# Decayed attention and a gated FFN on one core: a build-time list scheduler, q, k and x turned by DMA, paired heads, and a first batch in two parts

## The chip, the cores and the metric

The kernel runs on one core of one Trainium2 chip. Its time is the device time of one execution in microseconds (us). Every run below was timed together with runs of the kernel before on the same chip. "Span" is the length of the one execution that was profiled; it is some 2 us shorter than its time.

The names in the profile: PE is the matrix engine (TensorE) and PEld its weight loads, DVE is VectorE, ACT is ScalarE, POOL is GpSimd, SP is SyncE. "SPq" in a line of the profile stands for SP's queue, on which DMAs are issued.

## The reference, cut to what matters

```python
# q, k, v: [8 batches, 8 heads, 576 tokens, 64]; f: [8, 8, 576]
scores = scale * q @ k.T
decay  = cum[:, :, :, None] - cum[:, :, None, :]      # cum = cumsum(log f)
attn   = softmax(where(causal, -1e9, scores + decay))
x      = (attn @ v).transpose(0, 2, 1, 3).reshape(4608, 512)
xn     = x / sqrt(mean(x * x) + 1e-6) * rms_g
out    = (silu(xn @ w_gate) * (xn @ w_val)) @ w_out    # 512 -> 1536 -> 512
```

Attention of one batch must be done before the FFN can work on its 576 tokens. The FFN has groups of 512 tokens, so a batch's rows feed two groups.

## The kernel before

q and k arrive as [tokens, heads x 64] and have to be turned (transposed), so that the 64 features of a head lie on the partitions. PE does it, 128x128 at a time, and DVE copies the result out of PSUM. x is turned in the same way after the norm. Scores are made head by head, one 512-column bank at a time.

```python
def transposes(b, p):
    for src, store, nm in ((qb[b % 2], QT, "QT"), (kb[b % 2], KT, "KT")):
        tp = ps_tr.tile([128, NB * 128], BF16, name="tr")
        for j in range(NB):
            nc.tensor.transpose(tp[:, j * 128:(j + 1) * 128], src[:, j, p * 128:(p + 1) * 128], ident)
        t = store[b, p] = qkt.tile([128, NB * 128], BF16, name=f"{nm}{p}")
        nc.vector.tensor_copy(t, tp)

def scores(b, p, bank):
    for par in range(2):                       # the two heads of pair p
        # ... (cut)
        rows = slice(par * 64, par * 64 + 64)
        sc = ps_sc.tile([128, 512], F32, name="sc")
        for kj, q0, n, c in BANKS[bank]:
            nc.tensor.matmul(sc[:, c:c + n], lhsT=KT[b, p][rows, kj * 128:(kj + 1) * 128],
                             rhs=QT[b, p][rows, q0:q0 + n], start=True, stop=True)
        t = PT[b, h]
        nc.scalar.activation(t[:, bank * 512:(bank + 1) * 512], sc, ACT.Exp, scale=scale)
        # ... causal masks on POOL (cut)

def norm(b):
    # ... squares of the 5 row blocks on ACT, rs = (mean + eps) ** -0.5 on POOL (cut)
    for j in range(NB):
        nc.vector.tensor_scalar_mul(xn[:, j, :], x[:, j, :], rs[:, j:j + 1])
```

The order of the work is that of the program. All of batch 0's attention comes first. After it the attention pieces of batches 1 to 7 are spread between the FFN pieces by an estimate of their cost:

```python
for _, work in attention(0):
    work()
# ... stream = attention pieces of batches 1 to 7 with a cost each (cut)
for work in ffn:
    n += 1
    want = lead + total_a * n / (slots + LEAD)
    while i < len(stream) and done_a < want:
        done_a += stream[i][0]
        stream[i][1]()
        i += 1
    work[1]()
```

The softmax here doesn't subtract the row's maximum and nothing guards it: scores larger than these inputs give would overflow.

## Time and profile before

The time was 487.32 us (median of 3 runs, 486.21 to 487.49), and the profiled span 484.0 us. First four lines of the page of the kernel before: the engines' busy time, and then one digit for each of 40 equal slices of the span (12.1 us each). A digit is the busy share in tenths; in the PEclk line it is the granted clock of PE in tenths of full speed.

```profile
PE 423.9 (88%) x3317; PEld 207.6 (43%) x3317; DVE 260.3 (54%) x534; ACT 222.1 (46%) x436; POOL 187.7 (39%) x335
...
PE   0491707999999999999999999999999999999996
...
PEclk9999999999999999999999999999999999999999
DMA  9999991594190419041903290010001000201102
```

After the seventh slice PE is busy without a break. In the first six it is mostly idle, while the DMA engines are full. The view by stretches gives the same in numbers. Its columns are the stretch, its length, the busy time (and count) of PE, PEld, DVE, ACT and POOL, the granted clock, the DMA engines' mean load, and GB/s.

```profile
0.00:74.00 74.00, 28.48 (x239) 15.88 (x239) 17.75 (x49) 21.26 (x40) 57.63 (x95) 1.00 1.48 177
100.00:436.00 336.00, 327.60 (x2663) 160.06 (x2662) 209.16 (x426) 174.76 (x350) 119.37 (x221) 1.00 0.37 52
```

From 100 to 436 us PE is busy 327.6 of 336 us (97.5%): it is the bound there, and only less PE work can shorten it. In the first 74 us PE works 28.5 us. Its timeline shows how the head ends, and what attention costs PE later. A line has the start, the length, engine, line, operation, tiles, shapes and count, and in brackets the idle time before it with what ended it.

```profile
59.40 0.93 PE L231 MATMUL po<-Vs_104,PT 128*128 128x65 bf16 x14 [0.90 <-DVE x L235]
...
72.66 0.29 PE L258 MATMUL tr<-ident,xn 128*128 128x128 bf16 x1 [10.45 <-DVE xn L252]
...
75.89 0.58 PE L296 MATMUL ff<-xT,wg 128*128 128x512 bf16 x1 [0.58 <-DVE xT L265]
...
230.37 0.58 PE L202 MATMUL sc<-QT_2664,KT_2672 64*128 64x512 bf16 x2
...
235.50 0.59 PE L231 MATMUL po<-Vs_104,PT 128*128 128x65 bf16 x14
...
236.05 0.39 PE L202 MATMUL sc<-QT_2695,KT_2703 64*128 64x512 bf16 x2
```

The first FFN matmul is at 75.89 us, after PE waited 10.45 us for the normed rows of batch 0. Deep in the run two score banks of one pair (one 512-column matmul for each head) take 0.58 us at 230.37 us, where they run one after the other, and 0.39 us at 236.05 us, where they overlap.

**How PE time is split in this document.** I count the work of PE as each matmul's columns divided by 2.4, plus 2.5, in ns, and score matmuls of two paired heads as half, because they can run side by side. (Five small float32 matmuls at the start are counted four times, 0.4 us in all.) This is an estimate. The Trainium skill (TensorE: Matmul & The Clock Gate, Back-to-back issue gap) has this formula for isolated matmuls, and the trace of before agrees: 28 matmuls of 512 columns in a row took 6.04 us, 0.2157 us each. (For a stream of matmuls the same section gives about 131 ns at 512 columns; the trace doesn't show that.) Elapsed time less this work is called *loss*. For the kernel before, work is 279.7 (FFN) + 77.8 (attention) = 357.5 us, and the loss is 484.0 - 357.5 = 126.5 us: 82.8 before 140 us, 25.8 from 140 to 320 us, and 17.9 after that.

### The profile page before, as it was taken

The numbers are of one execution on the slowest core, as the hardware profiler recorded it, in microseconds if no ns is written. First come the engines' busy times: TensorE is split into PE (matmuls) and PEld (weight loads), VectorE is DVE, ScalarE is ACT, GpSimd is POOL, SyncE is SP. The second block draws the span as 40 slices with busy tenths as digits, with TensorE's granted clock in tenths as the row PEclk, the third lists the DMA queues.
The fourth block names the chain that finished last, engine by engine and source line by source line (L and its number), as shares of the span: only waits on it lengthen the run. The fifth ranks groups of instructions, "written<-read, shape, count | busy, mean of one in ns | idle before, by whom it ended". The sixth has DMA issues, their size and how long they took to land.

```text
span 484.0 us, 8505 instructions
## 1 busy us (share of the span) xinstructions
PE 423.9 (88%) x3317; PEld 207.6 (43%) x3317; DVE 260.3 (54%) x534; ACT 222.1 (46%) x436; POOL 187.7 (39%) x335
## 2 busy tenths in 40 slices
PE   0491707999999999999999999999999999999996
PEld 0231403454544454445444544454444544444442
DVE  3210326478447844784478457745774577373670
ACT  3060321664465437544754474447444744232321
POOL 8539990665182518252825282513111211000000
PEclk9999999999999999999999999999999999999999
DMA  9999991594190419041903290010001000201102
GB/s 151 175 195 178 191 187 33 36 65 99 65 120 3 100 66 119 3 100 67 120 1 77 70 118 0 1 66 23 3 0 66 23 1 0 88 1 45 43 1 87
DMA packets 123080, 33.73 MB, mean 70 GB/s; under 512 B 113760, under 2 KB 118368, under 8 KB 123040
## 3 DMA queue, kind: packets, MB, share of 16 engines
q0 software_dynamic: 79744, 14.16, 36.6%
q1 hardware_dynamic: 43296, 19.03, 14.9%
q8 instruction: 26, 0.43, 0.4%
q14 instruction: 14, 0.11, 0.1%
HBM read 37.90 MB, written 9.44 MB: 98 GB/s over the span
## 4 chain that ended last, share of the span: by engine, by line
PE 67%; POOL 13%; issue 6%; DMA 6%; ACT 5%; DVE 2%; POOLq 0%; ACTq 0%
PE ff L311 20%; PE ff L296 14%; PE ff L304 13%; PE sc L202 7%; PE po L231 5%; PE tr L167 4%; DMA wv<-in_moe_w_val_dram 3%; PE tr L258 3%; POOL Vs_104 L160 2%; DMA qb_100<-in_q_dram 2%; ACT junk L245 2%; POOL Vs_105 L160 2%; POOL rs L249 2%; ACT PT L205 2%; POOL qb_100 L77 2%
## 5 line engine op out<-in xcount | busy, mean ns | idle before, releaser
L205 ACT ACTIVATE PT<-sc 128x512 bf16<-128x512 f32 x192 | 105.1, 599 | 87.6 <-PE sc L202 73.8
L296 PE MATMUL ff<-xT,wg 128*128 128x512 bf16 x432 | 114.7, 382 | 0.7 <-DVE xT L265 0.6
L304 PE MATMUL ff<-xT,wv 128*128 128x512 bf16 x432 | 114.0, 380 | 0.0
L311 PE MATMUL ff<-wo,hT 128*128 128x512 bf16 x432 | 112.5, 380 | 0.0
L301 DVE SCALAR_TENSOR_TENSOR ga<-th,ff 128x512 f32<-128x512 f32 x108 | 74.2, 687 | 66.9 <-ACT th L299 66.3
L299 ACT ACTIVATE th<-ff 128x512 f32<-128x512 f32 x108 | 64.5, 598 | 82.6 <-PE ff L296 80.9
L306 DVE SCALAR_TENSOR_TENSOR hT<-ga,ff 128x512 bf16<-128x512 f32 x108 | 74.2, 687 | 9.0 <-PE ff L304 0.3
L304 PEld LDWEIGHTS <-wv 128*128 128x128 bf16 x432 | 42.2, 98 | 50.2 <-issue 2.5
L208 POOL TENSOR_SCALAR_AFFINE_SELECT PT<-PT 128x128 bf16<-128x128 bf16 x64 | 19.1, 299 | 97.8 <-ACT PT L205 97.6
L296 PEld LDWEIGHTS <-wg 128*128 128x128 bf16 x432 | 38.6, 98 | 42.0 <-issue 5.6
L314 ACT COPY ores<-ff 128x512 f32<-128x512 f32 x36 | 21.1, 586 | 75.2 <-PE ff L311 74.4
L213 POOL TENSOR_SCALAR_AFFINE_SELECT PT<-PT 128x384 bf16<-128x384 bf16 x64 | 33.0, 528 | 53.2 <-ACT PT L205 53.1
L311 PEld LDWEIGHTS <-hT 128*128 128x128 bf16 x432 | 36.5, 98 | 36.4 <-issue 9.5
L231 PEld LDWEIGHTS <-PT 128*128 128x128 bf16 x896 | 35.7, 102 | 31.2 <-POOL PT L208 9.7
L234 DVE RECIPROCAL rden<-po 128x5 f32<-128x5 f32 x64 | 12.2, 191 | 55.3 <-PE po L231 55.3
L258 PE MATMUL tr<-ident,xn 128*128 128x128 bf16 x160 | 20.6, 229 | 18.3 <-DVE xn L252 18.0
L231 PE MATMUL po<-Vs_104,PT 128*128 128x65 bf16 x448 | 22.7, 206 | 13.6 <-POOL PT L208 9.2
L235 DVE TENSOR_TENSOR x<-po,rden 128x320 f32<-128x320 f32 x64 | 31.4, 490 | 1.7
L245 ACT ACTIVATE junk<-x 128x512 bf16<-128x512 f32 x40 | 25.0, 624 | 9.0 <-DVE x L235 8.4
L258 PEld LDWEIGHTS <-xn 128*128 128x128 bf16 x160 | 12.4, 100 | 37.0 <-DVE xn L252 29.1
L265 DVE TENSOR_SCALAR xT<-tr,rg 128x512 bf16<-128x512 bf16 (+7 forms) x64 | 20.5, 362 | 12.3 <-PE tr L258 12.1
L252 DVE TENSOR_SCALAR xn<-x,rs 128x512 bf16<-128x512 f32 x40 | 18.1, 520 | 13.2 <-POOL rs L249 13.2
(300 smaller groups left out, 387.8 us busy)
## 6 DMA issues: line engine op xcount, KB each, us to landing
out_dram<-ores SPq DMA_DIRECT2D x36, 256.0 KB, 2.0
qb_100<-in_q_dram POOLq DMA_DIRECT2D x16, 128.0 KB, 5.3
kb_102<-in_k_dram POOLq DMA_DIRECT2D x16, 128.0 KB, 5.4
qb_101<-in_q_dram POOLq DMA_DIRECT2D x16, 128.0 KB, 4.4
kb_103<-in_k_dram POOLq DMA_DIRECT2D x16, 128.0 KB, 4.5
wg<-in_moe_w_gate_dram POOLq DMA_DIRECT2D x3, 512.0 KB, 12.7
wv<-in_moe_w_val_dram POOLq DMA_DIRECT2D x3, 512.0 KB, 14.0
wo<-in_moe_w_out_dram POOLq DMA_DIRECT2D x2, 768.0 KB, 12.3
```

Of the source, the lines that this page charges most:

```text
L202: nc.tensor.matmul(sc[:, c:c + n], lhsT=KT[b, p][rows, kj * 128:(kj + 1) * 128], rhs=QT[b, p][rows, q0:q0 + n], start=True, stop=True)
L205: nc.scalar.activation(t[:, bank * 512:(bank + 1) * 512], sc, ACT.Exp, scale=scale)
L213: nc.gpsimd.affine_select(out=d, in_=d, pattern=[[0, 3], [1, 128]], compare_op=ALU.is_ge, fill=0.0, base=0, channel_multiplier=-1)
L231: nc.tensor.matmul(po[:, qi, :], lhsT=weights_of(b, h, qi, kj), rhs=Vs[b % 2][:, kj, h, :], start=(kj == 0), stop=(kj == qi))
L245: nc.scalar.activation(junk, x[:, j, :], ACT.Square, accum_out=sq[:, j:j + 1])
L258: nc.tensor.transpose(tp[:, j * 128:(j + 1) * 128], xn[:, j, dc * 128:(dc + 1) * 128], ident)
L296: nc.tensor.matmul(pg, lhsT=wg[:, dc, fc * 128:(fc + 1) * 128], rhs=xT[:, dc, :], start=(dc == 0), stop=(dc == NDC - 1))
L299: nc.scalar.activation(t, pg, ACT.Tanh, scale=0.5)
L301: nc.vector.scalar_tensor_tensor(a, in0=t, scalar=1.0, in1=pg, op0=ALU.add, op1=ALU.mult)
L304: nc.tensor.matmul(pv, lhsT=wv[:, dc, fc * 128:(fc + 1) * 128], rhs=xT[:, dc, :], start=(dc == 0), stop=(dc == NDC - 1))
L306: nc.vector.scalar_tensor_tensor(hTs[g][:, fc, :], in0=a, scalar=0.5, in1=pv, op0=ALU.mult, op1=ALU.mult)
L311: nc.tensor.matmul(po, lhsT=hTs[g][:, fc, j * 128:(j + 1) * 128], rhs=wo[:, fc, :], start=(fc == 0), stop=(fc == NFC - 1))
```

## The change

The intent: give PE less to do in the middle, and start the FFN sooner. The diff rewrites the kernel; these are its main parts.

1. All work is cut into pieces, each with an engine, a duration, dependencies and buffers. A list scheduler simulates the run at build time, and the program is written in the simulated order.
2. q and k (batches 1 to 7) and x are turned by DMAs that transpose, issued on SP's queue. Only batch 0 is still turned by PE (`PE_TURN`).
3. Two heads are made in one visit, with their matmuls alternating, and one exponential covers both (1024 columns).
4. The first batch is split in two parts, and the first two groups have 256 tokens, so that the FFN can begin on its first 256.

```diff
-LEAD = 6
+LEAD, UNTIL = 34.0, 0.85
+SPLIT, PE_TURN = (0,), (0,)
+GROUPS = ((0, 256), (256, 512)) + tuple((a, a + 512) for a in range(512, B * S, 512))
+LOAD_AHEAD, LOAD_LATE, SV_PRIO = -1.6, 0.3, -0.7
 ... (cut)
+class Plan:
+    def run(self):                     # a simulation in time; pieces go out in order of p.start
 ... (cut)
+        if e == "PE":
+            behind = a_done < self.lead + (a_total - self.lead) * min(1.0, f_done / (f_total * self.until))
+            first = "A" if behind else "F"                  # attention or FFN first
+            p = min(c, key=lambda p: (p.kind != first, p.prio))
 ... (cut)
+        dma_free = max(dma_free, p.start + 0.4 * p.dur) + p.xfer
+        p.done = max(dma_free, p.end) + 1.7
 ... (cut)
-            nc.tensor.transpose(tp[:, j * 128:(j + 1) * 128], src[:, j, p * 128:(p + 1) * 128], ident)
-        nc.vector.tensor_copy(t, tp)
+        def turn_dma(nm, j):
+            nc.sync.dma_start_transpose(out=QK[i][:, :, "qk".index(nm), j * 128:j * 128 + n],
+                                        in_=T[nm, b, j][0:n, :])
+        c = plan.add(key, "SP", 1.25 if j < 4 else 0.7, ..., xfer=0.8 if j < 4 else 0.4, ...)
 ... (cut)
+        for p, (c0, blocks, _) in visit:                    # two banks a visit
+            sc = ps_sc.tile([128, 2, 512], F32, name="sc", tag="sc")
+            for kj, q0, n, c in blocks:
+                for par in range(2):
+                    nc.tensor.matmul(sc[:, par, c:c + n], lhsT=QK[i][r, p, 1, ...], rhs=QK[i][r, p, 0, ...])
+        nc.scalar.activation(T["pt", b, p][:, :, c0:c0 + n], sc[:, :, 0:n], ACT.Exp, scale=scale)
 ... (cut)
+            nc.vector.scalar_tensor_tensor(xn, in0=x[:, j, :], scalar=rs[:, j:j + 1], in1=rgb, ...)
 ... (cut)
+with tc.manual_schedule():
+    for p in plan.run():
+        p.fn()
```

`UNTIL` is the share of the FFN over which attention is spread: at 0.85, the last attention piece is due when 85% of the FFN is done.

## The prediction

> **What bounds it now.** The span is 484.0 us (timed 487.3). By stretches: from 0 to 74 us PE is busy 28.5 us only and no FFN matmul runs (the timeline has the first at 75.9 us); DMA is saturated (share 1.48), POOL busy 57.6 us with load issues (0.88 us each), V scaling and masks; the waits show PE and ACT waiting for POOL masks (9.2 and 12.6 us) and PE for the first xn (11.3 us). From 100 to 436 us PE is busy 97.5% at full clock: it is the bound. There one batch takes 48.0 us (195 to 243), of which FFN is 144 matmuls of 512 columns at 0.2157 us (28 in a row: 6.04 us) = 31.1 us, so attention costs PE 16.9 us.
>
> **What the change does to PE.**
> - Turning q, k, x by DMA takes 60 PE transposes a batch away: groups of five cost 0.28 to 0.38 us in the timeline, so 4 to 4.5 us, plus about 1 us of waits for xn.
> - Paired heads: where both heads are adjacent now, two banks take 0.32 us; apart, each takes 0.32. The Trainium skill (TensorEngine Tiling, Overview) says that 64-row contractions can run as two independent tiles; the trace agrees where they meet. Two paired banks a visit: 2 x 0.213 + 0.1 = 0.53 us, six visits: 3.2 us a batch against about 6.
> - Values stay: 0.46 us a head, 3.7 us. The last corner: 0.25 us.
> So attention is about 7.2 us a batch for 1 to 7, saving 9.7 x 7 = 68 us on the critical engine. PE's sum: 280 (FFN) + 8 x 7.2 + about 5 (batch 0's transposes and split) = 343 us.
>
> **Head.** 256-token groups and the split batch let FFN begin about 25 us; weights (landing by about 35 us now) pace group 0. Groups 0 and 1 are 31 us of PE. Group 2 needs batch 1: loads land about 55 us, its 12 exponentials of about 1.04 us (two 0.6 us ones joined) bound that stretch, with some of batch 2's, so group 2 begins about 80 us. PE idle up to there: 26 to 32 us (45 now).
>
> **Costs added.** About 16 DMA transposes a batch on SP's queue (HWDGE only, by the skill's DMA: Bandwidth & Descriptors, DMA Transpose; no trace shows one yet). I take 1 to 1.5 us each: 16 to 24 us of SP in a 39 us batch. Loads now take a DMA share of 0.56 of 48 us = 27 us, so the queues are near full; SP in order may hold back v loads and stores. ACT (26 us), DVE (25) and POOL (22) fit in 39 us.
>
> **Sum.** By 82 us PE has done about 54 of 343 us; 289 remain, plus 3% of stalls (9) and 4 us of last copy and store: span 384, timed 388 us. Range 368 to 422. Faster by over 2%: 0.95; within 2%: 0.02; slower: 0.03.
>
> **Right or wrong in the profile.** PE instructions fall from 3317 to about 3030; no PE transposes after 60 us; over 95% busy PE in slices from 85 us on; two-bank score visits about 0.53 us; first FFN matmul at 22 to 32 us; idle PE between groups 1 and 2, released by ACT exponentials or DMA transposes; DMA transposes landing in 2 to 4 us.
>
> **What would make it wrong.** DMA transposes of 3 us or more each on SP, which would make the queue the bound (130 x 3 = 390 us); PE waiting on DMA or POOL in mid-span because the build-time order misses the real durations; score pairs not overlapping (plus 20 us); a starved start (FFN after 40 us).

## The result, and the profile after

| | kernel before | kernel after |
|---|---|---|
| time, median (5 runs) | 487.14 us (486.21 to 487.49) | 444.67 us (442.0 to 445.16) |
| span of the profiled run | 484.0 us | 440.3 us |
| PE work, as estimated above | 357.5 us | 334.1 us |
| loss up to 140 us / 140 to 320 us / 320 us to the end | 82.8 / 25.8 / 17.9 us | 74.4 / 9.3 / 22.6 us |

The ratio is 0.9129, with a 95% interval of 0.9102 to 0.9155. Ratios and intervals in this document are from the fast runs of the same rounds; they are not quite the ratio of the medians. The change saves 42.5 us; the prediction was 388 us, with 422 us as the upper end. Of the 43.7 us of span, 23.4 us is less PE work and 20.3 us is less loss. The work is mostly the transposes that PE no longer does (e5 below, which gives them back to PE, has 21.2 us more). What pairing brings is part of the loss, since the estimate counts score matmuls as half in both kernels.

The same four lines of the page of the kernel after (a slice is 11.0 us here), and one line from its list of DMA issues (tiles, queue, operation, count, median us from issue to landing):

```profile
PE 372.5 (85%) x3033; PEld 195.8 (44%) x3033; DVE 236.0 (54%) x446; ACT 213.3 (48%) x351; POOL 191.3 (43%) x283
...
PE   0468829974589999998999999999999952999996
...
PEclk9999968995589999999999999999999985899999
DMA  9999999999999999999990621100220112101002
...
QK<-ld SPq DMA_TRANSPOSE x70, 4.4
```

PE begins sooner, but falls back twice in the head, in the sixth slice and from the ninth to the eleventh, and there is a new hole near the end (the 5 and the 2). The DMA engines are full for 21 slices, up to 231 us, where before they were full for six and then in bursts. The 70 DMA transposes of q and k are new, and land 4.4 us after their issue in the median of the whole run. The view by stretches of the kernel after:

```profile
0.00:127.00 127.00, 80.13 (x892) 53.94 (x893) 55.76 (x140) 60.65 (x99) 97.44 (x150) 0.87 1.64 158
127.00:340.00 213.00, 209.39 (x1692) 103.43 (x1689) 137.44 (x239) 121.45 (x200) 90.36 (x130) 1.00 0.81 105
340.00:380.00 40.00, 26.56 (x198) 13.10 (x197) 13.27 (x26) 13.95 (x24) 3.54 (x4) 0.79 0.18 42
```

The middle is 98% busy, as hoped. PE's timeline of the kernel after, head, middle and tail:

```profile
37.05 1.04 PE L670 MATMUL ff<-xT,wg 128*128 128x256 bf16 x4
...
63.56 1.27 PE L577 MATMUL ff<-ident,xn 128*128 128x128 bf16 x8 [5.84 <-DVE xn L552]
...
81.57 0.61 PE L495 MATMUL sc<-QK 64*128 64x128 bf16 x8
...
119.29 0.93 PE L524 MATMUL po<-Vs,PT 128*128 128x65 bf16 x14 [3.08 <-DVE x L533]
...
127.08 1.03 PE L670 MATMUL ff<-xT,wg 128*128 128x512 bf16 x4
...
252.10 0.61 PE L495 MATMUL sc<-QK 64*128 64x128 bf16 x8
252.64 1.04 PE L670 MATMUL ff<-xT,wv 128*128 128x512 bf16 x4
...
371.68 1.87 PE L670 MATMUL ff<-xT,wg 128*128 128x512 bf16 x4 [9.29 <-issue]
```

The FFN begins at 37.05 us instead of 75.89. Batch 1's first scores are at 81.57 us, and group 2, the first that needs batch 1 (the first gate matmul of 512 columns), begins at 127.08 us. Up to there PE has done 53.8 us of work and lost 73.3 us, to waits as the 3.08 us before 119.29 and to slow matmuls as those of that line (14 value matmuls in 0.93 us). In the middle, a visit of two paired banks takes from 252.10 to 252.64 us, so 0.54 us up to the next matmul. At the end PE waits 9.29 us before 371.68 us and then runs four gate matmuls in 1.87 us instead of 1.04: at half clock.

What held batch 1? SP's queue in the timeline of the kernel after (a run of issues is one line; its second number is the time from the first one's start to the last one's end):

```profile
42.41 3.70 SPq L440 DMA_TRANSPOSE QK<-ld  x2
...
49.58 16.00 SPq L440 DMA_TRANSPOSE QK<-ld  x5
...
66.29 9.57 SPq L440 DMA_TRANSPOSE QK<-ld  x4
...
116.55 7.84 SPq L571 DMA_TRANSPOSE xT<-xn  x6
```

Batch 1's ten q and k loads are issued on POOL from 25.6 to 49.1 us, and land 10.8 to 16.9 us later. The transposes that follow them then take 16.00 us for five and 9.57 us for four on SP, and land 7.3 to 14.2 us after their issue in this stretch (median 9.4). That is why the first scores are at 81.57 us: the last block that they need lands at 78.6 us. From 40 to 180 us SP's queue has few gaps: DMA issues fill 34.8 of 40, 46.5 of 50 and 46.4 of 50 us (40 to 80, 80 to 130 and 130 to 180 us). Batch 1's attention ends at 105.4 us (its last product on DVE), and DVE starts on its first normed rows at 111.90 us. The six transposes of its x come on SP only at 116.55 us, behind nine of batch 3's q and k, and take 7.84 us; the four that group 2 needs have landed by 126.3 us, and then it begins.

The clock matters too. The Trainium skill (TensorE: Matmul & The Clock Gate, Part 1) says that the granted clock falls to half after an idle window of about 3.4 us and comes back after a busy one. The clock record of the kernel after agrees on the length of the window: it has three stretches at 0.50, from 59.1, 100.0 and 359.5 us, of 10.2, 23.9 and 17.1 us, which are 3, 7 and 5 times 3.41 us, and in them matmuls take about twice as long. It differs on "idle": the second and the third began before PE's long waits. In the 3.41 us ahead of each PE had been busy 42% and 47% of the time, with no gap longer than 1 us:

```profile
96.63:100.04 3.41, 1.45 (x32) 1.01 (x32) 0.69 (x2) 3.32 (x4) 2.77 (x4) 1.00 1.73 191
356.04:359.45 3.41, 1.59 (x40) 1.22 (x39) 1.37 (x4) 2.01 (x3) 1.51 (x2) 1.00 0.00 0
```

So short gaps close together were enough here to lose the clock. By the estimate above the three stretches cost 11.9 us in all. Before 38.6 us the trace holds no clock event, and the views show 1.00; but there matmuls are as slow as at half clock (four gate matmuls of 256 columns at 37.05 us take 1.04 us, and 0.60 us at 79.95 us), which costs some 6.6 us more by the same estimate. It is not all a cost of the change: the kernel before ran its head at half clock as well (0.93 us against 0.59 us for 14 value matmuls, shown above), some 10.8 us up to its first clock event at 79.4 us.

### The profile page after: what moved, and what is told of

The parts are those of the page before. It is cut to its first block, busy times and chain, and to the rows that moved or that the text cites. A ratio compares the mean times of both kernels' runs of the same rounds, so it can differ in the third digit from the quotient of the medians.

```text
span 440.3 us, 7998 instructions
## 1 busy us (share of the span) xinstructions
PE 372.5 (85%) x3033; PEld 195.8 (44%) x3033; DVE 236.0 (54%) x446; ACT 213.3 (48%) x351; POOL 191.3 (43%) x283
## 3 DMA queue, kind: packets, MB, share of 16 engines
q1 hardware_dynamic: 94912, 31.69, 42.0%
## 4 chain that ended last, share of the span: by engine, by line
PE 63%; DVE 9%; DMA 9%; POOL 7%; issue 6%; ACT 3%; SPq 2%; POOLq 0%; DVEq 0%; ACTq 0%
PE ff L670 33%; PE ff L691 20%; PE po L524 6%; PE sc L495 3%; DVE xn L552 3%; DMA ld<-in_q_dram 3%; DMA v<-in_v_dram 3%; DVE x L533 2%; DVE ga L679 2%; POOL Vs L367 2%; DMA ld<-in_k_dram 2%; DVE hT L685 2%; SPq L440 1%; DMA out_dram<-ores 1%; POOL ld L349 1%
## 5 line engine op out<-in xcount | busy, mean ns | idle before, releaser
L670 PE MATMUL ff<-xT,wg 128*128 128x512 bf16 (+1 forms) x480 | 116.0, 365 | 9.9 <-issue 9.3
L670 PE MATMUL ff<-xT,wv 128*128 128x512 bf16 (+1 forms) x480 | 115.1, 363 | 2.8 <-DVE ga L679 2.6
L675 ACT ACTIVATE th<-ff 128x512 f32<-128x512 f32 (+1 forms) x120 | 66.4, 554 | 96.0 <-PE ff L670 93.3
L503 ACT ACTIVATE PT<-sc 128x1024 bf16<-128x1024 f32 (+2 forms) x100 | 94.6, 989 | 36.0 <-PE sc L495 35.2
L679 DVE SCALAR_TENSOR_TENSOR ga<-th,ff 128x512 f32<-128x512 f32 (+1 forms) x120 | 75.8, 631 | 61.1 <-ACT th L675 60.6
L511 POOL TENSOR_SCALAR_AFFINE_SELECT PT<-PT 128x1024 bf16<-128x1024 bf16 (+1 forms) x44 | 37.8, 872 | 120.3 <-ACT PT L503 119.7
L685 DVE SCALAR_TENSOR_TENSOR hT<-ga,ff 128x512 bf16<-128x512 f32 (+1 forms) x120 | 76.1, 634 | 18.7 <-PE ff L670 6.8
L524 PE MATMUL po<-Vs,PT 128*128 128x65 bf16 x896 | 43.2, 202 | 17.5 <-DVE x L533 16.3
L552 DVE SCALAR_TENSOR_TENSOR xn<-x,rs,rgb 128x512 bf16<-128x512 f32 x40 | 35.4, 928 | 31.4 <-POOL rs L548 31.4
L495 PE MATMUL sc<-QK 64*128 64x64 bf16 (+3 forms) x584 | 35.9, 257 | 10.7 <-ACT PT L503 7.1
L349 POOL DMA_DIRECT2D ld<-in_k_dram x40 | 34.8, 870 | 6.9 <-DMA QK<-ld 5.2
## 6 DMA issues: line engine op xcount, KB each, us to landing
wo<-in_moe_w_out_dram POOLq DMA_DIRECT2D x2, 768.0 KB, 18.1
```

What stands on the lines that cost most here:

```text
L349: nc.gpsimd.dma_start(out=t[0:block(j), :].rearrange("p (h d) -> p h d", d=D), in_=src[b, :, j * 128:j * 128 + block(j), :].rearrange("h p ...
L495: nc.tensor.matmul(sc[:, par, c:c + n], lhsT=QK[i][r, p, 1, kj * 128:(kj + 1) * 128], rhs=QK[i][r, p, 0, q0:q0 + n], start=True, stop=True)
L503: nc.scalar.activation(T["pt", b, p][:, :, c0:c0 + n], T.pop(("sc", b, p, c0))[:, :, 0:n], ACT.Exp, scale=scale)
L524: nc.tensor.matmul(po[:, qi, :], lhsT=w, rhs=Vs[i][:, kj, h, :], start=(kj == 0), stop=(kj == qi))
L552: nc.vector.scalar_tensor_tensor(xn, in0=T["x", b][:, j, :], scalar=T["rs", b, js][:, j:j + 1], in1=rgb, op0=ALU.mult, op1=ALU.mult)
L670: nc.tensor.matmul(ps[:, 0:w], lhsT=wt[:, dc, fc * 128:(fc + 1) * 128], rhs=T["xT", g][:, dc, 0:w], start=(dc == 0), stop=(dc == NDC - 1))
```

## The experiments

The theories, as the expectations name them or imply them:

- **A**: turning batch 1's q, k and x by DMA is what makes group 2 late, because SP's queue and the DMA engines are full there.
- **The order (O)**: the list scheduler believes in a DMA that is too fast, so its order is wrong; an order planned with a slower DMA would be better. Its rival **Q**: a wrong idea of the DMA in either direction parks engines behind work that isn't ready.
- **The tail**: the hole at 362 to 371 us is mainly the exposed norm of the last batch, not its DMA transposes.
- **S or D**, about the mechanism of A: is it SP's issue time (S), or the time of the DMA engines (D)?

Every run was correct. The times of the kernel before in the same rounds had medians of 486.4 to 487.6 us. "Loss" is computed as above. The traces of six runs (e1, e2, e3, e4, e10, e11) lack some 40 of about 3030 matmul records, so their losses aren't given.

### e1_batch1_pe: batch 1 turned by PE as well

```diff
-SPLIT, PE_TURN = (0,), (0,)
+SPLIT, PE_TURN = (0,), (0, 1)
```

> Batch 1's q, k and x are turned on PE (as batch 0's are), all else as in the changed kernel. Theory A (the DMA transposes of batch 1, queued behind a saturated DMA and SP's in-order queue, set when FFN group 2 can begin): the first 512-wide gate matmul moves from 127 us to 105 us or earlier, and the time falls from 444.7 to 420-432 us. Rival B (the head is held by the loads of q, k, v and the weights and by POOL, the transposes ride along): group 2 begins within 6 us of 127 us and the time stays within 440-450 us.

Measured: 438.25 us (436.62 to 439.4), ratio 0.9007 (0.8974 to 0.904). Group 2 begins at 112.1 us instead of 127.1, though not at 105 us or earlier, as A had expected:

```profile
112.12 1.04 PE L670 MATMUL ff<-xT,wg 128*128 128x512 bf16 x3
```

So batch 1's DMA transposes do delay group 2, by 15 us. The run moves q, k and x together, and the two traces tell them apart: batch 1's attention ends 6.4 us sooner (98.98 against 105.37 us), and from the start of its first normed rows to group 2 it takes 6.8 us instead of 15.2. More than half of the 15 us is thus x, not q and k.

But the whole run gains 6.4 us only. The rest is given back later: the last rows of group 6 are still copied out 12.7 us sooner than in the kernel after (306.2 against 318.9 us), those of group 7 only 1.5 us sooner (352.3 against 353.8). In between PE waits 4.13 us for an exponential at 312.7 us, and the recorded clock is at half from 309.9 to 320.1 us. The hole before the last batch's x is what it was (9.25 us before 367.9 us, against 9.29). A's expected total was missed.

### e2_load_late: q and k loads later

```diff
-LOAD_AHEAD, LOAD_LATE, SV_PRIO = -1.6, 0.3, -0.7
+LOAD_AHEAD, LOAD_LATE, SV_PRIO = -1.0, 0.3, -0.7
```

> The q and k loads of each later batch get a later priority (-1.0 instead of -1.6 batches ahead), so that fewer loads compete with batch 1's loads and transposes in the head. Theory A' (contention of early loads for the same DMA engines): group 2 begins 5 to 15 us before 127 us and the time is 430-440 us. Rival (the loads are needed when they come; order is not the matter): the time rises to 445-460 us or stays within 2 us.

Measured: 455.16 us (453.07 to 456.04), ratio 0.9347 (0.9318 to 0.9376). This experiment failed: the number also moved batch 0's loads behind the weights, so the first FFN matmul came at 57.8 us, and nothing follows for batches 2 and 3. It was mended as e7.

### e3_batch7_pe: batch 7 turned by PE as well

```diff
+SPLIT, PE_TURN = (0,), (0, 7)
```

> Only the last batch's q, k, x are turned on PE besides batch 0's. Theory T (the 9.3 us hole at 362 us and the slow clock after it come from the last batch's norm and DMA transposes of x, with no FFN work left to fill it): the hole falls below 6 us and the time by 3 to 8 us, to 437-442 us. Rival (the hole is the norm chain on ACT, POOL and DVE, the transposes are 1 or 2 us of it): the time moves by less than 3 us.

Measured: 445.55 us (444.38 to 448.51), ratio 0.9165 (0.9128 to 0.9201); against 0.9129 for the kernel after, nothing is gained. A hole of 6.91 us stays near the end, now with PE waiting for DVE's normed rows. So the DMA transposes aren't the main part of the tail's hole. What fills it in the kernel after is the norm of the last batch, a chain over three engines. Its timeline there, one engine's line after the other:

```profile
363.19 0.63 ACT L539 ACTIVATE junk<-x 128x512 bf16<-128x512 f32 x1 [5.13 <-DVE x L533]
...
367.29 1.17 POOL L548 TENSOR_TENSOR rs<-ms,mhalf 128x5 f32<-128x5 f32 x1
...
368.49 3.40 DVE L552 SCALAR_TENSOR_TENSOR xn<-x,rs,rgb 128x512 bf16<-128x512 f32 x5 [5.33 <-POOL rs L548]
```

Five squares on ACT from 363.19 us, the power on POOL up to 368.46 us, and the first of five norms on DVE (3.40 us for all five), which ends at about 369.2 us. The next group needs only that first block; its DMA transpose takes the time to 371.68 us, when PE goes on. So of the wait of 9.29 us some 2.5 us is the DMA transpose (an estimate from these lines), which agrees with the 6.91 us that e3 leaves, and the rest is the norm, at a moment when no FFN work is left that doesn't need it. What e3 gained in the hole it paid for elsewhere.

### e6_until_70: attention spread over 70% of the FFN

```diff
-LEAD, UNTIL = 34.0, 0.85
+LEAD, UNTIL = 34.0, 0.70
```

> Attention is to be done when 70% of the FFN work is done instead of 85%. Theory T (the 18 us lost between 340 and 380 us come from the last batch's attention finishing just before its FFN group is due, so that nothing is left to fill its norm chain): that loss falls under 6 us and the time by 8-14 us, to 431-437 us. Rival (attention cannot come earlier because loads or exponentials hold it): PE stalls appear elsewhere and the time moves by less than 4 us.

Measured: 433.61 us (431.67 to 434.74), ratio 0.8905 (0.8871 to 0.8939). The loss after 320 us falls from 22.6 to 5.3 us, by 17.3 us; that from 140 to 320 us rises from 9.3 to 18.1 us (one wait of 3.20 us for a copy on POOL at 239.5 us, among others), so a part is given back here too. With the attention done earlier, there is FFN work to put beside the last norm. The view by stretches of this run shows a tail with PE 97% busy at full clock:

```profile
320.00:432.00 112.00, 108.32 (x573) 49.57 (x571) 56.99 (x89) 38.37 (x67) 3.55 (x4) 1.00 0.13 44
```

One constant was worth 11 us.

### e4_no_split: the first batch in one part

```diff
+SPLIT, PE_TURN = (), (0,)
```

> Batch 0 is worked whole instead of in two parts (groups stay 256, 256, 512...). If the split head is worth what it was meant to be, the first FFN matmul moves from 37 us to 55-62 us. Theory A says that group 2 at 127 us is bound by batch 1 and the DMA, not by group 0, so the time changes by less than 8 us (440-452 us). Rival (the head is bound by PE work that has to be done early): the time rises by 10 to 20 us.

Measured: 457.5 us (456.21 to 460.71), ratio 0.9411 (0.9368 to 0.9454); the first FFN matmul is at 60.4 us instead of 37.1. So the split is worth 13 us. It works, also in a head that is otherwise limited by the DMA; the guess that it would be worth under 8 us was wrong.

### e5_all_pe: no transposes of q, k or x by DMA at all

```diff
+SPLIT, PE_TURN = (0,), (0, 1, 2, 3, 4, 5, 6, 7)
```

> No DMA transposes at all: every batch's q, k and x are turned on PE. PE gains some 3.3 us of transposes a batch for batches 1 to 7 (23 us over the kernel, read at full clock). Theory A (transposes crowd the DMA, which in the changed kernel's profile is busy in 9 tenths up to about 250 us, and delay batches 1 and 2): the loss of PE time in the first 140 us falls by 15 us or more, so that the total is 430-446 us in spite of the added PE work. Rival (loads and serial chains hold the head, DMA transposes are nearly free): the time rises by 15-25 us, to 458-470 us.

Measured: 462.09 us (461.16 to 463.62), ratio 0.9503 (0.9477 to 0.9529). The PE and DMA slices of its page:

```profile
PE   0468869999999989999899999999779982999996
...
DMA  9999999998896157024009401051100020001102
```

The head is what A says: the DMA engines are full for nine slices and nearly so for three more, instead of 21, PE is 80% busy or more from the seventh slice to the 28th, group 2 begins at 112.2 us, and the loss up to 140 us falls by 15.4 us to 59.0. The total is worse all the same: PE has 21.2 us more work, and the tail loses 31.7 us. Turning by DMA is a gain of 17 us over the whole run (462.09 - 444.67), though a loss in the head. A's expected total was missed here too: the time fell in the rival's range.

### e7_b2_later: only the loads of batches 2 and later moved

```diff
-prio=(b + LOAD_AHEAD + 0.01 * j + late,)
+prio=(b + (LOAD_AHEAD if b < 2 else -1.0) + 0.01 * j + late,)
```

> Mends e2, which moved batch 0's and batch 1's loads as well: only from batch 2 on are the q and k loads issued later (-1.0 batches instead of -1.6). Theory A' (early loads of batches 2 and 3 crowd out batch 1's transposes): the first 512-wide gate matmul comes 5 to 15 us before 127 us, the time is 430-441 us. Rival (the DMA is not what holds batch 1): it stays within 4 us of 127 us and the time within 5 us of 444.7 us, or is longer as later batches starve.

Measured: 442.98 us (442.31 to 445.69), ratio 0.9117 (0.9084 to 0.9151), and group 2 at 127.6 us: no change. Early loads of batches 2 and 3 don't crowd out batch 1.

### e8_slow_dma_plan and e11_fast_dma_plan: another DMA in the scheduler's model

```diff
-dma_free = max(dma_free, p.start + 0.4 * p.dur) + p.xfer
+dma_free = max(dma_free, p.start + 0.4 * p.dur) + 1.6 * p.xfer      # e8; e11 has 0.6 *
```

(In e11 one dependency was added, so that the norm's power can't be put ahead of the piece that sets its exponent.)

> Only the build-time plan's idea of a transfer's time is changed: 1.6 times longer. The instructions are the same, their order alone differs. Theory O (the plan takes DMA to be faster than it is, so that PE, POOL and SP, which work in order, are parked behind transfers that have not landed, as at 23-25 us): the first FFN matmul comes 3 to 6 us before 37 us, the loss before 140 us falls by 5-15 us, the time is 430-440 us. Rival (the order is right, the transfers themselves are what holds): less than 4 us either way.

> The opposite of e8: the plan takes a transfer to be 0.6 times as long (and the one dependency that this order needs, of the first power on the constant tile's memset, is added). e8, at 1.6, gave 487 us against 444.7 us from order alone. Theory P (an optimistic plan issues loads and attention early, which the in-order engines can absorb, a pessimistic one postpones attention and leaves FFN groups without input): 435-445 us. Theory Q (the measured order sits at an optimum, and any wrong idea of DMA time parks engines): 455-490 us, with more PE waits on DMA and POOL.

Measured: e8 487.08 us (484.95 to 487.85), ratio 1.0006 (0.9977 to 1.0036), the same as the kernel before. e11 455.41 us (453.91 to 456.68), ratio 0.9363 (0.9327 to 0.9398). The instructions are those of the kernel after, apart from their order, and with e8's order the whole gain of the change is gone. PE's slices of e8, and a line of its PE timeline:

```profile
PE   1338739955173999998799999989978993699996
```

```profile
416.63 1.89 PE L670 MATMUL ff<-xT,wg 128*128 128x512 bf16 x4 [9.25 <-DMA xT<-xn]
```

In e8 the first FFN matmul came 2.7 us sooner, and everything else later: group 2 at 147.3 us, holes in the middle, and the last attention after 400 us. So O is wrong, at this factor at least. In e11 the first FFN matmul came at 75.1 us, since DVE waited 33.0 us, up to 71.7 us, for the norm's power on POOL. On POOL the power came behind pieces that waited 8.4 us for a load of v, and behind the constant that the added dependency names, which this order sets at 69.3 us (at 10.9 us in the kernel after). An engine works in order, so one piece placed too early stops everything behind it. Both times are as Q expected, but e11 has the added dependency beside its new order, so Q rests on e8. Why the two orders cost just 42 and 11 us wasn't taken apart.

### e10_apart: the two heads of a visit one after the other

```diff
-for kj, q0, n, c in blocks:
-    for par in range(2):            # head 0, head 1, head 0, head 1 ...
+for par in range(2):
+    for p, (c0, blocks, _) in visit:        # all of head 0's, then all of head 1's
```

> Undoes the pairing alone: all of the first head's score matmuls of a visit come before all of the second head's, so that the two row halves meet only at one boundary. A two-bank visit should go from 0.53-0.55 us to about 0.95 us. If pairing is worth on the clock what the prediction gave it where PE is the bound (about 0.4 us x 6 visits x 7 batches = 17 us, less what idle PE in the head hides, some 5 us), the time rises by 8-16 us to 453-461 us. Rival (PE's idle time or its overlap with weight loads hides it): less than 4 us.

Measured: 446.01 us (445.69 to 447.44), ratio 0.9177 (0.9152 to 0.9202): 1.3 us slower, where 8 to 16 had been expected. Two visits in PE's timeline of this run, each with the line that follows it:

```profile
243.35 0.88 PE L497 MATMUL sc<-QK 64*128 64x384 bf16 x14
244.16 5.35 PE L693 MATMUL ff<-wo,hT 128*128 128x512 bf16 x23
...
255.55 0.62 PE L497 MATMUL sc<-QK 64*128 64x128 bf16 x8
256.10 1.04 PE L672 MATMUL ff<-xT,wv 128*128 128x512 bf16 x4
```

A visit of 8 matmuls takes 0.55 us in this order as well (255.55 to 256.10). The visits of 14 matmuls take longer, 0.65 or 0.81 us by the order of their blocks (243.35 to 244.16) instead of 0.55. The Trainium skill (TensorEngine Tiling, Overview) says that matmuls with 64 rows of contraction can run as two independent tiles. The trace agrees, and shows more: where each head has four matmuls in a row, PE overlaps the two halves by itself (the eight start in pairs, 13 or 14 ns apart). The alternation in the source is worth little. The run thus doesn't take the overlap away, as it was meant to, and what it is worth to have both heads in one visit stays unmeasured.

### e13_double_turn: every DMA transpose of q and k issued twice

```diff
+extra = xp.tile([128, NP, 128], BF16, name="extra", tag="extra", bufs=3)
+nc.sync.dma_start_transpose(out=extra[:, :, 0:n], in_=T[nm, b, j][0:n, :])
```

The second one goes to a spare tile. The plan, and so the order on the other engines, is the same.

> Every DMA transpose of q and k is issued twice, the second time into a spare tile that nobody reads; the plan does not know of it, so the order on PE, ACT, DVE and POOL stays. Theory A (transposes by DMA are what holds batches 1 and 2 in the head): the first 512-wide gate matmul moves from 127 us to 140 us or later and the time rises by 12 us or more, to 457-475 us. Rival (they have slack): less than 5 us.

Measured: 514.91 us (513.63 to 515.44), ratio 1.0563 (1.0536 to 1.059), far more than A had expected. The 70 added transposes cost 70 us, 1.0 us each; group 2 begins at 154.8 us. The durations of the added issues in this run (ns, minimum/median/maximum) beside those of the kernel after:

```profile
L443 SPq DMA_TRANSPOSE extra<-ld x70: 1196/1257/2824, 43.7 to 329.8; - x70
```

```profile
L440 SPq DMA_TRANSPOSE QK<-ld x70: 1187/1217/5610, 42.4 to 254.3; - x70
```

So the added transposes are not hidden, as A says. But the copies also hold the loaded tiles longer, and POOL waited 70.6 us in all for them before its next loads (8.5 us for the transposes in the kernel after), so the 70 us can't be put down to SP's queue alone:

```profile
POOL ld L349 <- DMA extra<-ld: 70.6, 32, 5.5
```

### e15_tiny_dma: a 128-byte DMA behind every transpose

```diff
+tiny = xp.tile([1, 32], F32, name="tiny", tag="tiny", bufs=8)
+nc.sync.dma_start(out=tiny, in_=<32 floats of the gains>)
```

This adds issue time on SP, and next to nothing for the DMA engines to move.

> Behind each DMA transpose of q and k, SP issues one plain DMA of 128 bytes from DRAM into a spare tile (order on the other engines unchanged). It costs SP some 0.5 to 0.6 us of issue each, 35 to 42 us in all, next to nothing of the DMA engines' time. Theory S (SP's issue time is the bound between 40 and 250 us; e13's 1.0 us for each added transpose is issue): the time rises by 18-40 us, to 463-485 us. Theory D (the DMA engines, or the landing of the transposes, are the bound): less than 8 us.

Measured: 456.67 us (454.2 to 459.27), ratio 0.9374 (0.9321 to 0.9427). The added issues in this run:

```profile
L443 SPq DMA_DIRECT2D tiny<-in_moe_rms_g_dram x70: 411/422/458, 43.9 to 271.4; - x70
```

That is 70 x 0.42 = 29.5 us of SP, and it cost 12 us of time, about 0.4 of it. This lies between what S and D expected (18 to 40 us, and under 8 us). SP's issue time is a part of the cost of a transpose. How the rest divides between the DMA engines and the tiles held is left open.

### e9_pe1_until70, e12_pe1_until70_again, e14_pe1_until60: the two cures together

```diff
-LEAD, UNTIL = 34.0, 0.85
-SPLIT, PE_TURN = (0,), (0,)
+LEAD, UNTIL = 34.0, 0.70            # e14: 0.60
+SPLIT, PE_TURN = (0,), (0, 1)
```

> e1 and e6 together: batch 1 turned on PE and attention done at 70% of the FFN. If the head's loss (theory A) and the tail's hole (theory T) are separate, the gains add: 444.7 - 6.4 - 11.1 = 427 us, 423-431 us. If they are the same reserve of FFN work moved about, the time stays at 432-436 us.

> The kernel of e9 once more, because its profiled execution took 1306 us (every matmul about four times as long) while its three timed ones took 414.1 to 415.2 us. If that execution was an accident of the chip, all runs are 412-417 us and the profile shows the loss before 140 us below 60 us and after 320 us below 8 us. If the kernel itself can fall into that state, it happens again. The sum 414.8 us is 12 us below what e1's and e6's gains add up to; theory: e1's later holes (308-312 us, 357-368 us) are gone here as well.

> As e9 with attention done at 60% of the FFN. If the tail's hole is closed already at 70%, nothing is left there and the time stays at 413-419 us, or rises by 2-6 us because attention is pressed into a stretch in which exponentials and loads set the pace.

Measured: e9 414.12, 414.38 and 415.15 us in its timed runs, ratio 0.8524 (0.85 to 0.8549), but 1306.91 us in its profiled one, which the run lists as slow. e12 is the same kernel again: 414.45 us (412.85 to 415.34), ratio 0.8494 (0.8466 to 0.8523), with no slow run. e14: 414.89 us (414.76 to 416.69), ratio 0.8523 (0.8498 to 0.8547): moving the attention forward still more brings nothing.

This version beats both kernels: 30 us under the kernel after, 73 us under the kernel before. It is also better than the sum of the two cures (6.4 + 11 = 17.4 us), so e9's expectation of 423 to 431 us was missed on the good side. The losses below show why: the head loses 12.3 us less than in the kernel after, the tail 17.7 us less, and the middle is as it was, where e1 and e6 each gave a part of their gain back. The page of e12, its last stretch, and its group 2:

```profile
PE 371.0 (90%) x3093; PEld 194.7 (47%) x3093; DVE 236.8 (57%) x454; ACT 214.4 (52%) x355; POOL 190.2 (46%) x283
...
PE   1477849996699999999899999999999999999996
...
PEclk9999985999599999999999999999999999999999
```

```profile
320.00:414.00 94.00, 89.47 (x439) 40.60 (x436) 50.60 (x77) 29.92 (x55) 1.49 (x3) 1.00 0.12 41
```

```profile
63.88 1.03 PE L495 MATMUL sc<-QK 64*128 64x128 bf16 x8 [0.37 <-DVE QK L416]
...
112.83 1.42 PE L670 MATMUL ff<-xT,wg 128*128 128x512 bf16 x4
```

Batch 1's scores come at 63.88 us instead of 81.57, and group 2 at 112.83 instead of 127.08. The loss is 62.1 us up to 140 us, 9.5 to 320 us and 4.9 after that, against 74.4, 9.3 and 22.6 in the kernel after. Of e12's expectation, a head's loss under 60 us was just missed, and a tail's under 8 us was met. The head is still the largest loss.

The slow execution of e9 isn't explained. A line of PE's timeline in it:

```profile
602.05 3.52 PE L670 MATMUL ff<-xT,wg 128*128 128x512 bf16 x4
```

Four gate matmuls, 1.04 us in a fast run, took 3.52 us. PE was slow throughout (1248.3 us busy), while DVE, ACT and POOL were busy as long as in e12. Its trace holds no clock event, so the 1.00 that the run lists says nothing. It came once, in one of more than 60 executions of kernels of this family, and no conclusion here uses it.

## Why the prediction was right or wrong

The direction was right, and the sum was too low by 56 us of span (384 against 440.3). The prediction's 384 us was 343 us of work, 28 us of idle PE before group 2 (82 - 54), and 13 us of stalls and end. The run had 334.1 us of work, 73.3 us of loss before group 2, and 106.2 - 73.3 = 32.9 us of loss after it. So -9 + 45 + 20 = 56.

**The step that failed most: "so group 2 begins about 80 us", with "PE idle up to there: 26 to 32 us".** It began at 127.08 us, with a loss of 73.3 us. The work done by then was as predicted (53.8 us against 54); only the wait was mis-sized. Its terms:

- "Loads land about 55 us": batch 1's loads were issued until 49.1 us and took 10.8 to 16.9 us to land, so the last landed at 63.2 us.
- "I take 1 to 1.5 us each" for the transposes, "landing in 2 to 4 us". At best an issue takes 1.19 us, but from 40 to 80 us thirteen of them took 31.1 us, 2.4 us each, and landed 7.3 to 14.2 us later. They were costed alone, for a queue that is used by loads, stores and transposes at once, and for DMA engines that were full already. The prediction had named the danger ("3 us or more each on SP") and had written that "the queues are near full", but had put no time for it in the head's sum.
- The head was said to be bound by exponentials. e1 and e12 show that 14 to 15 us of it are batch 1's DMA transposes, of q, k and x. The norm of batch 1 and the turning of its x have no term in the sum at all: from the end of its attention to group 2 they took 21.7 us (105.4 to 127.08).

The first FFN matmul was expected about 25 us (22 to 32), and came at 37.05 us; what held it wasn't taken apart. That it starts so early is worth 13 us (e4).

**The clock was left out.** Three recorded stretches at half clock cost 11.9 us (an estimate, as explained): 8.4 us of it before group 2, 3.5 us in the tail, and the time before the first clock event some 6.6 us more. Idle PE was counted once in the prediction, and the slow matmuls after it not at all.

**"Plus 3% of stalls (9) and 4 us of last copy and store" was too small for the tail.** From 340 to 380 us the loss alone was 18.1 us. The cause is not in the middle: it is the exposed norm of the last batch (from the squares at 363.19 us to the first norm, 6 us, and a DMA transpose after it), with half clock behind it. e3 shows that without the transposes 6.91 us stay and no time is won; e6 shows that spreading the attention over 70% of the FFN removes it.

**What held.** PE's work: 343 us predicted, 334.1 found. PE instructions: about 3030 predicted, 3033 found. Two-bank visits: 0.53 us predicted, 0.54 found. Joined exponentials: 1.04 us predicted, 1.02 found. PE transposes end at 66 us (60 predicted). Busy PE in the middle: over 95% predicted from 85 us on, 98% found, but from 127 us on. That the mid-span would be bound by PE and not by DMA was right: the DMA engines were full up to 231 us, and after the head PE waited for a transfer only in the tail's hole (some 2.5 of its 9.29 us). The fear that "the build-time order misses the real durations" was right in kind: e8 shows that an order alone can cost all of the gain.

One added cost was not seen. The norm now multiplies by the gains as well, so DVE reads two inputs from SBUF: 0.75 us alone, and up to 2.13 us (0.48 us median, at most 1.27 us, before). The Trainium skill (SBUF — State Buffer, Who interferes with whom) says that such a DVE instruction contends with a GpSimd instruction that reads SBUF. The trace agrees: where a computation of POOL runs beside them, the median is about 1.1 us, and 0.75 us elsewhere. No run takes this apart from the rest.

Still open: what pairing the heads is worth; how the cost of a transpose divides between SP's issue time and the DMA engines; why e8's and e11's orders cost just what they do; and the 1307 us execution.

## What to carry to other kernels

When work is moved from a busy engine to a DMA queue, cost it at the load that the queue has there: here the same transposes were a gain of 17 us over the run and a loss of 15 us in the head, where the queue was full, and the best version moved only those of the batches that weren't urgent. Look for the place where a gain in one stage is given back: one cure brought 6 us, the other 11, and both together 30. A build-time order is as much a part of the kernel as its instructions, so try its few constants on the chip, since one of them took 11 us off the time and another put 42 us on.

## What the Trainium skill lacked or had wrong

- Advanced Engine Details and Errata, X-Bar Transpose (TRN2): it says that "TRN2 transpose DMAs are as fast as regular DMAs". The runs differ for small ones. A 128 KB transpose within SBUF keeps SP's queue for 1.19 us at least (median 1.22), where a plain 256 KB load of v has a median of 0.53 us. The packets of the queue that SP fills took 42.0% of 16 engines' 440.3 us for 31.69 MB in the kernel after, and 16.8% of 461.9 us for 19.29 MB in e5, which has no DMA transposes: by this estimate some 8.7 us a MB for the transposes, crowded as they were, against 4.0. And each added transpose cost 1.0 us of the run's time (e13).
- DMA: Bandwidth & Descriptors, DMA Transpose (X-bar): it gives constraints and, elsewhere on the page, bandwidths and sequencer cycles, but not how long one instruction holds the issuing queue when the DMA engines are full. Here it was 2.4 us each from 40 to 80 us, at most 5.61 us, with 7.3 to 14.2 us to landing instead of 2.3 us at best.
- TensorEngine Tiling (Array Packing): it doesn't say how near to each other the matmuls of two row tiles must be in the program to overlap. Here four and four in a row overlapped as well as alternating ones (0.55 us both ways), and seven and seven did not quite (0.65 or 0.81 against 0.55 us).
- TensorE: Matmul & The Clock Gate, Part 1: it ties the half clock to an idle window and gives no figure for how little idle time is enough. In the kernel after the clock fell after windows of 3.41 us in which PE was busy 42% and 47% of the time.
- TensorE: Matmul & The Clock Gate, Part 1: it warns that the recorded clock events can't be fully trusted. Here they were missing: there is none before 79.4 us in the kernel before, where 14 value matmuls took 0.93 us instead of 0.59. It tells of a quarter clock for over 50 us; in one execution here, without any clock event, four gate matmuls at 602 us took 3.52 us instead of 1.04, and PE was slow over all of 1305 us. Whether it was that state isn't shown.
